# Attention feeding a hash-routed expert layer: a new start order, and one expert's gathers issued earlier

## The chip, the cores and the metric

The kernel runs on one core of a Trainium2 chip. The metric is the device time of one execution in microseconds. All times below are microseconds from the start of the profiled span unless a duration is meant. Engines: TensorE (PE in the profile; PEld is its weight load), VectorE (DVE), ScalarE (ACT), GpSimd (POOL) and SyncE (SP). POOL and SP also issue DMA transfers; those of POOL share one queue, q0.

## The reference

```python
# attention: batch 8, 12 heads, 448 tokens, head width 64
q_n, k_n = rmsnorm(q, g_q), rmsnorm(k, g_k)          # x / sqrt(mean(x*x) + 1e-6) * g
attn = softmax(q_n @ k_n.T / sqrt(64))
x = (attn @ v) as rows of 768                        # 3584 tokens
# experts: 8, width 768 -> 1024 -> 768
e = token_id * 2654435761 % 8
out[token] = relu(x[token] @ w1[e]) @ w2[e]
```

## The kernel before

**Attention.** The 96 heads are taken in 48 steps of two heads; a batch has 6 steps. A step needs the square sums of its q and k rows (`sqq`, `sqk`, then `sumq`, `sumk` on TensorE against the identity, then `redq`, `redk` on VectorE), the factor 1/rms (`ln`, `er`, two small ScalarE operations), the scaled rows (`nq`, `nk`, VectorE), their transposes (`Tq`, `Tk`, TensorE) and the copies of these into SBUF (`qT`, `kT`). Then come four score products (`sc`), four exponentials on ScalarE (`exp`), the product with v (`av`), the row sums (`rec`) and the scaling (`x`). Factors are made per group: group 0 is step 0, group 1 is steps 1 and 2, group 2 is steps 3, 4 (its first part, `sqk:2.0.0`) and 5 (`sqk:2.0.1`).

Every engine works through its instructions in program order, and that order is written out by hand: `emit` reads a text of tokens (`kind:step.part`). The first text covers batches 0 and 1, the texts `steady` and `tail` the rest. `@A` puts an operation on ScalarE, `@S` takes a score bank for a result. `spin:n` emits n products of zeros whose result nobody reads.

**The first loads.** The lines 803 to 821 issue them: step 0 over several queues, then on POOL's queue k and q of steps 1 and 2 (`load_pairs(..., 1, 0, ...)`), v of steps 0 to 2 (`load_v(0, 3)`, four transfers), k and q of steps 3 and 4, v of steps 3 to 5, and then whole batches. Step 5 comes over SP's queue (`load_one`).

**Experts.** For expert e, `gemm1` makes the hidden rows of 512 token slots and `gemm2` the output rows, tile by tile (4 tiles of 128 slots; the last has 96). The tokens of expert e are gathered from the stored attention result by `fetch(e, ...)`, four indirect transfers issued by POOL; `xg_ring` holds two experts' tokens. They are turned by TensorE (`turn`, experts 0 and 1) or by 16 VectorE instructions for a whole expert (`turn_blocks`, experts 2 to 6), which read all four tiles at once. The weights of expert 3 and later are a list of five pieces each, `queue`; `w_next` issues pieces between other work on POOL. In the loop over e the order on POOL is: `fetch(e + 2)`, pieces, then four scatters of the output, each followed by a piece:

```python
if e < E - 2:
    fetch(e + 2, range(KT))
    turn_blocks(e + 1)
gemm1(w1_view(e, w1_sb), xTs.pop(e), h_sb, 0, FIT, e >= E - 2, after)
...
(0, "k", 2): [table_mm, lambda: fetch(2, range(KT))],
```

The last line is an entry of `plan`, run behind the third tile of expert 0's `gemm2`.

Of the kernel before, what the change touches and what calls it, by code (L numbers as in the profile page):

```python
# [20 lines left out]
def kernel(  # L21
# [14 lines left out]
    B, H, S, D = q.shape  # L36
# [4 lines left out]
    HP = H // 2  # L41
# [10 lines left out]
    LAST = FIT - 3 * P  # L52
    KT = CAP // P
# [211 lines left out]
    with tc.manual_schedule(), \  # L265
# [15 lines left out]
        q_bufs = [qk_keep[0], a_nat.tile([P, RAW], FP16, name="qr_1")]  # L281
# [32 lines left out]

        def load_pairs(t, bufs, b, h, o, step, n):
            dst = raw_at(bufs, b, o, n * SL * D).rearrange("p (n r) -> p n r", n=n)
            nc.gpsimd.dma_start(out=dst, in_=bass.AP(
                tensor=t.tensor, offset=t.offset + (b * H + h) * S * D,
                ap=[[SL * D, P], [step * S * D, n], [1, SL * D]]))

        def load_v(s, n):
            b = s // HP
            o = HP * (b % 2) + s % HP
            load_heads([nc.gpsimd] * 4, v_bufs[b // 2 % NB][:, o:o + n], v, s, n)
# [480 lines left out]
        setup()  # L805
        nc.vector.memset(warm, 0.0)
        load_pairs(k, k_bufs, 0, 1, 0, HP, 2)
        make_identity(nc, ident16[:])
        load_pairs(q, q_bufs, 0, 1, 0, HP, 2)
        load_v(0, 3)  # L810
        load_pairs(k, k_bufs, 0, 3, 2 * PAIR, HP, 2)
        load_pairs(q, q_bufs, 0, 3, 2 * PAIR, HP, 2)
        load_v(3, 3)
        load(1)
        load(2, "kq")
# [72 lines left out]
        def emit(text, b):  # L888
# [15 lines left out]
                    step_ops[kind](s0 + at, *rest)  # L904

        emit("""
            zero:0 zero:1 zero:2 zero:6 zero:7 spin:11 sqk:0.0 zero:3 sqq@A:0.0 sumk@S:0.0
            redk:0.0 sumq@S:0.0 ln:0.1.2 redq:0.0 er:0.1.2 ln:0.0.1 er:0.0.1 sqk@A:1.0
            gain:0 spin:2 nk:0 spin:4 gain:1 Tk@S:0 nq:0 sumk@S:1.0 gain:2 sqq:1.0 Tq@S:0
            redk:1.0 sumq:1.0 kT:0 redq:1.0 qT@A:0 sc:0.0 ln:1 er:1 sc:0.1 spin:5 exp:0.0  # L910
            nk:1 Tk@S:1 sc:0.3 nq:1 Tq:1 sqk:2.0.0 kT:1 qT:1 exp:0.1 sqq:2.0.0 v:0
            sqk@A:2.0.1 sc:0.2 exp:0.3 sumk@S:2.0 sc:1.0 sqq@A:2.0.1 exp:0.2 exp:1.0
            sumq:2.0 redk:2.0 av:0.0 redq:2.0 sc:1.2 av:0.1 v:1 sc:1.3 ln:2 er:2 av:0.2
            sc:1.1 nq:3 rec:0 exp:1.2 exp:1.3 Tq@S:3 exp:1.1 nk:3 sc:2.0 Tk:3 x:0 exp:2.0
            sc:2.1 exp:2.1 qT:3 kT:3 sc:2.2 av:1.0 exp:2.2 sc:2.3 av:1.1 av:1.2 sqk:3.0
            sc:4.0 exp:2.3 nk:5 sumk:3.0 rec:1 exp:4.0 sc:3.0 x:1 sc:3.1 av:2.0 redk:3.0
            av:2.1 sqk:4.0 exp:3.0 nq:5 sumk:4.0 v:2 sc:3.2 av:2.2 redk:4.0 sqq:3.0 rec:2
            exp:3.1 Tk@S:5 sc:3.3 kT:5 x:2 sumq:3.0 exp:3.2 sc:4.3 sc:4.2 exp:3.3 redq:3.0
            exp:4.3 ln:3 er:3 sc:4.1 exp:4.2 av:3.0 sqk:4.1 Tq:5 exp:4.1 sqq:4.0 av:3.1 qT:5
            sumk@S:4.1 nq:6 av:3.2 nk:6 redk:4.1 sc:5.0 rec:3 sumq:4.0 sc:5.3 sc:5.1 exp:5.0  # L920
            exp:5.3 redq:4.0 sqq:4.1 x:3 Tk:6 exp:5.1 Tq@S:6 kT:6 sumq@S:4.1 redq:4.1 qT@A:6
            av:4.0 av:4.1 ln:4 sc:5.2 av:4.2 er:4 exp:5.2 sc:6.0 sqk:5.0 v:4 sc:7.0 sumk:5.0
            exp:6.0 rec:4 sc:6.3 x:4 av:5.0 av:5.1 exp:7.0 exp:6.3 nq:8 sc:7.3 redk:5.0 nk:8
            exp:7.3 v:3 Tq:8 sc:6.1 av:5.2 qT:8 sc:6.2 Tk@S:8 rec:5 sqq:5.0 exp:6.1 sc:7.1
            sumq:5.0 x:5 exp:6.2 av:6.0 sc:7.2 exp:7.1 exp:7.2 kT:8 sc:8.0 sqq:5.1 redq:5.0
            sc:8.1 nq:10 exp:8.0 av:6.1 sumq:5.1 nk:10 redq:5.1 exp:8.1 av:6.2 sc:8.3 rec:6
            Tk:10 x:6 sc:9.0 sc:8.2 exp:8.3 av:7.0 sc:9.3 exp:9.0 kT:10 Tq:10 av:7.1 av:7.2
            sc:9.1 sqk:5.1 qT:10 exp:8.2 rec:7 sc:9.2 x:7 v:5 exp:9.3 exp:9.1 sumk:5.1
            redk:5.1 exp:9.2 sqq:6.0 av:8.0 av:8.1 av:8.2 sc:10.0 sc:10.2 sc:10.1 rec:8 ln:5
            er:5 x:8 nk:12 exp:10.0 sumq:6.0 av:9.0 exp:10.1 sc:10.3 redq:6.0 Tk:12 av:9.1  # L930
            nq:12 av:9.2 kT:12 rec:9 exp:10.2 sc:11.0 exp:10.3 exp:11.0 sc:11.2 exp:11.2
            sc:11.3 x:9 Tq:12 sqq:6.1 av:10.0 av:10.1 sc:11.1 qT:12 nk:14 av:10.2 exp:11.3
            sc:12.0 sumq:6.1 sc:12.2 rec:10 exp:11.1 sc:12.1 x:10 exp:12.0 exp:12.2 redq:6.1
            Tk:14 sc:12.3 sqk:6.0 exp:12.1
        """, None)
        steady = """
            exp:0.3 av:-1.0 av:-1.1 nq:2 av:-1.2 kT:2 sc:1.0 exp:1.0 rec:-1 x:-1 Tq:2 sc:1.1
# [26 lines left out]
    with tc.manual_schedule(), \  # L964
# [83 lines left out]
        def fetch(e, kts):  # L1048
            for kt in kts:
                c = e * KT + kt  # L1050
                xgs[c] = gather(xg_ring[:, c % (2 * KT)],
                                gidx[0:P if kt < KT - 1 else LAST, c:c + 1],
                                N_EARLY if kt < KT - 1 else N)
# [4 lines left out]
            bank = ps_x.tile([P, DIN], FP16, name="xT_ps")  # L1058
            put_xT(xgs.pop(e * KT + kt), xTs[e], kt, bank[:], copy)

        def turn_blocks(e):
            xT = xTs[e] = m_x.tile([P, CO, CAP], FP16, name="xT")
            c0 = e * KT % (2 * KT)
            xg = xg_ring[:, c0:c0 + KT].rearrange("p k (c m r) -> p k m c r", m=4, r=32)
            dst = xT[:].rearrange("p c (g r) -> p c g r", r=32)
            for kt in range(KT):
                xgs.pop(e * KT + kt)
            for i in range(4):
                n = KT if 32 * i < LAST else KT - 1
                g = slice(i, i + 4 * (n - 1) + 1, 4)  # L1070
                for m in range(4):
                    nc.vector.transpose(  # L1072
                        out=dst[32 * m:32 * m + 32, :, g].rearrange("p c k r -> p k c r"),
                        in_=xg[32 * i:32 * i + 32, 0:n, m])
# [166 lines left out]
        def each(f, *parts):  # L1241
            return [lambda p=p: f(p) for p in parts]
# [3 lines left out]
            (0, "g", 4): [p7, p8], (0, "g", 5): [p9, p10, p11],  # L1246
            (0, "g", 6): each(low, 0, 1), (0, "g", 7): each(low, 2, 3), (0, "k", 0): [high],
            (0, "k", 1): [high_tok], (0, "k", 2): [table_mm, lambda: fetch(2, range(KT))],
            (1, "k", 0): [overflow_table],
        }  # L1250
        t = lambda e, kt: (lambda: turn(e, kt))
        t0 = lambda e, kt: (lambda: turn(e, kt, nc.scalar.copy))
        before, between = {}, {}
# [10 lines left out]
        for e in range(E):  # L1264
            w1_sb, w2_sb = w_tiles[e]
            h_sb = hs[e] = m_h.tile([P, FO, CAP], FP16, name="h_sb")
            after = [plan.get((e, "g", fo), []) for fo in range(FO)]
            if e == 0:
                gemm1(w1_view(e, w1_sb), xTs[e], h_sb, 0, EARLY, False, after, 2)
            else:  # L1270
                if e == E - 2:
                    turn_by_dma(E - 1)
                if e < E - 2:
                    fetch(e + 2, range(KT))
                    turn_blocks(e + 1)
                gemm1(w1_view(e, w1_sb), xTs.pop(e), h_sb, 0, FIT, e >= E - 2, after)
            if e:
                w_next(2)
            if e == 2:
                n_ov = nc.values_load(novi[0:1, 0:1], min_val=0, max_val=NOV)  # L1280
            if e == E - 1:
                nc.gpsimd.drain()
            for kt in range(KT):
                c = e * KT + kt
                for f in before.get((e, kt), []):
                    f()
                gemm2(w2_sb, h_sb, kt, gidx[:, c:c + 1], between=between.get((e, kt)),
                      last=(c == E * KT - 1), by_v=e in (0, E - 2, E - 1))
                for f in plan.get((e, "k", kt), []):
                    f()  # L1290
                if e or kt > 1:
                    w_next(1)
            w_next(len(queue))
            if e + 4 < E:
                queue += w_pieces(e + 4)
# [47 lines left out]
```

## Time and profile before

| | |
|---|---|
| median of 3 runs (lowest to highest) | 333.07 us (332.08 to 333.38) |
| the profiled execution: time, span | 332.74 us, 331.1 us |
| PE busy | 318.2 us (96%) |
| VectorE busy | 239.3 us (72%) |
| ScalarE busy | 207.5 us (63%) |
| POOL busy | 149.5 us (45%) |
| POOL's DMA queue q0 | 39072 packets, 58.32 MB |

Attention lasts to about 160 us, the experts from there to the end. Between two instructions of an engine the trace notes the idle time in brackets and what ended it, as `[0.52 <-DVE xT L1072]`. A row with `xN` merges N instructions in sequence.

### The profile page before, as it was taken

To read this page: it belongs to the slowest core of one execution; us is meant where nothing else is said; L and a number is where in the kernel's file an instruction comes from. 1 tells how busy PE (TensorE), PEld (TensorE's weight loads), DVE (VectorE), ACT (ScalarE), POOL (GpSimd) and SP (SyncE) were. 2 spreads that over 40 slices of the span, in tenths; PEclk is the share of its full clock that TensorE was granted. 3 is DMA by queue.
4 is the path that set the end of the run, shared out by engine and by line. 5 is a ranking of instruction groups with operands and counts; after the bars stand their busy time and mean duration, and the time that the engine had idled before them with its cause. 6 is when DMAs were issued, how large, how long until landed. Compare 5 with 4: busy or idle time off the path is not lost. (4 is left out here: it accounts for less than half of the span.)

```text
span 331.1 us, 8985 instructions
## 1 busy us (share of the span) xinstructions
PE 318.2 (96%) x3765; PEld 219.7 (66%) x3765; DVE 239.3 (72%) x457; ACT 207.5 (63%) x317; POOL 149.5 (45%) x207
## 2 busy tenths in 40 slices
PE   7699999999999999999999999999999999999992
PEld 3467777777777777666767766666676675766761
DVE  4689999898999999985694397693958939422210
ACT  4699999999999999999543333424334253321211
POOL 8799944432441100003475872655727556403122
PEclk9999999999999999999999999999999999999997
DMA  6999999999999999722478699999999999993013
GB/s 122 197 202 203 194 242 196 236 200 240 203 240 212 245 225 227 164 70 70 124 152 211 165 207 242 244 264 265 265 272 239 254 253 260 307 174 137 23 48 124
DMA packets 45601, 65.52 MB, mean 198 GB/s; under 512 B 12727, under 2 KB 33423, under 8 KB 45432
## 3 DMA queue, kind: packets, MB, share of 16 engines
q0 software_dynamic: 39072, 58.32, 87.7%
q1 hardware_dynamic: 6328, 6.50, 7.5%
q8 instruction: 30, 0.49, 0.6%
q10 hardware_dynamic: 160, 0.11, 0.1%
q14 instruction: 11, 0.09, 0.1%
HBM read 89.29 MB, written 17.30 MB: 322 GB/s over the span
## 5 line engine op out<-in xcount | busy, mean ns | idle before, releaser
L660 ACT ACTIVATE expT<-sc_ps 128x896 bf16<-128x896 f32 x144 | 125.1, 960 | 1.0 <-PE sc_ps L637 0.7
L1072 DVE STREAM_TRANSPOSE xT<-kr 32x768 f16<-32x768 f16 (+1 forms) x80 | 73.6, 920 | 25.7 <-DMA kr<-x_scratch,gidx 15.2
L1024 PEld LDWEIGHTS <-h_sb 128*128 128x128 f16 (+1 forms) x512 | 52.2, 104 | 31.3
L1024 PE MATMUL o_ps<-w_sb,h_sb 128*128 128x512 f16 (+3 forms) x384 | 64.2, 326 | 0.0
L1011 ACT ACTIVATE h_sb<-h_ps 128x480 f16<-128x480 f32 (+1 forms) x56 | 31.3, 560 | 48.6 <-PE h_ps L1002 48.6
L1037 POOL DMA_INDIRECT out_dram<-o_sb,gidx x32 | 35.1, 1097 | 57.6 <-ACT o_sb L1034 29.6
L1034 ACT COPY o_sb<-o_ps 128x768 f32<-128x768 f32 (+1 forms) x26 | 20.8, 799 | 54.5 <-PE o_ps L1024 54.5
L230 POOL DMA_INDIRECT kr<-x_scratch,gidx x32 | 32.6, 1020 | 49.3 <-DVE qT L629 37.1
L1002 PEld LDWEIGHTS <-w_sb 128*128 128x128 f16 x300 | 39.8, 135 | 16.4 <-issue 0.7
L1002 PE MATMUL h_ps<-xT,w_sb 128*128 128x480 f16 x240 | 49.4, 366 | 0.3 <-DVE xT L1072 0.3
L637 PE MATMUL sc_ps<-qT,kT 64*128 64x448 f16 x288 | 44.4, 356 | 0.5 <-DVE qT L629 0.4
L678 PEld LDWEIGHTS <-expT 128*128 128x128 bf16 x846 | 36.8, 97 | 9.2 <-DVE x_sb L738 4.4
L678 PE MATMUL av_ps<-v,expT 128*128 128x65 bf16 x828 | 41.5, 193 | 0.1
L306 POOL DMA_DIRECT2D vr<-in_v_dram x36 | 23.7, 670 | 20.8 <-DMA kr<-in_k_dram 11.5
L738 DVE TENSOR_TENSOR x_sb<-av_ps,srec 128x448 f16<-128x448 f32 x47 | 29.3, 623 | 1.3
L663 ACT ACTIVATE expT<-sc_ps 128x448 bf16<-128x448 f32 x48 | 28.4, 595 | 0.1
L387 PEld LDWEIGHTS <-ident 128*128 128x128 f16 x576 | 22.6, 98 | 8.7 <-issue 4.4
L683 PE MATMUL av_ps<-v,expT 128*128 128x130 bf16 x138 | 24.0, 220 | 0.0
L1024 PE MATMUL o_ps<-kr,h_sb 128*128 128x512 f16 (+3 forms) x128 | 21.1, 326 | 0.0
L1002 PE MATMUL h_ps<-xT,qr 128*128 128x480 f16 x96 | 19.8, 366 | 0.5 <-DVE xT L1072 0.5
L637 PEld LDWEIGHTS <-kT 64*128 64x128 f16 x288 | 12.3, 93 | 9.5 <-issue 2.2
L1105 POOL DMA_DIRECT2D w_sb<-in_moe_w_dram x20 | 13.7, 692 | 9.4 <-DMA w_sb<-in_moe_w_dram 6.8
(226 smaller groups left out, 409.4 us busy)
## 6 DMA issues: line engine op xcount, KB each, us to landing
w_sb<-in_moe_w_dram POOLq DMA_DIRECT2D x18, 512.0 KB, 12.5
w_sb<-in_moe_w_dram POOLq DMA_DIRECT2D x8, 768.0 KB, 12.7
kr<-in_k_dram POOLq DMA_DIRECT2D x7, 672.0 KB, 15.6
qr<-in_q_dram POOLq DMA_DIRECT2D x7, 672.0 KB, 12.9
x_scratch<-x_sb SPq DMA_DIRECT2D x15, 288.0 KB, 6.4
w_sb<-in_moe_w_dram POOLq DMA_DIRECT2D x2, 1536.0 KB, 21.3
qr<-in_moe_w_dram POOLq DMA_DIRECT2D x6, 512.0 KB, 17.6
vr<-in_v_dram POOLq DMA_DIRECT2D x14, 192.0 KB, 13.6
```

The lines of the kernel that those rows point to most:

```text
L230: nc.gpsimd.indirect_dma_start(out=xg[0:idx.shape[0], :], out_offset=None, in_=x_dram[0:rows, :], in_offset=bass.IndirectOffsetOnAxis(ap=i ...
L637: nc.tensor.matmul(sc[:, hh, :S], lhsT=kT[64 * hh:64 * hh + 64, P * j:P * j + P], rhs=qT[64 * hh:64 * hh + 64, :], start=True, stop=True)
L660: nc.scalar.activation(expT[:, 2 * j:2 * j + 2, :], sc[:, :, :S], AF.Exp, bias=0.0, scale=1.0)
L663: nc.scalar.activation(expT[:, 6, :], sc[:, 0, :S], AF.Exp, bias=0.0, scale=1.0)
L678: nc.tensor.matmul(av[:, 2 * t + hh, :], lhsT=expT[:, tl(hh, j), P * t:P * t + P], rhs=v8[:, i, vs(hh, j), 0:D + 1], start=(hh == 0 and t ...
L683: nc.tensor.matmul(av[:, 2 * t:2 * t + 2, :], lhsT=expT[:, 6, P * t:P * t + P], rhs=v8[:, i, 0::7, 0:D + 1], start=False, stop=False)
L738: nc.vector.tensor_tensor(out=xs[b][:, :, hp * D:hp * D + D], in0=av[:, :, :D], in1=srec[:, :, None].to_broadcast([P, SL, D]), op=ALU.mult)
L1002: nc.tensor.matmul(dst, lhsT=w1v[:, co, fo, :], rhs=src, start=(co == 0), stop=(co == CO - 1))
L1011: nc.scalar.activation(h_sb[:, fo, c0:c1], h_ps[:, :c1 - c0], AF.Relu)
L1024: nc.tensor.matmul(o_ps[d0 > 0][0:w, d0:d1], lhsT=h_sb[:, fo, col * P:col * P + w], rhs=w2_sb[:, fo, d0:d1], start=(fo == 0), stop=(fo == ...
L1037: scat = nc.gpsimd.indirect_dma_start(out=out[:, :], out_offset=bass.IndirectOffsetOnAxis(ap=idx[0:w], axis=0), in_=o_sb[0:w], in_offset=N ...
L1072: nc.vector.transpose(out=dst[32 * m:32 * m + 32, :, g].rearrange("p c k r -> p k c r"), in_=xg[32 * i:32 * i + 32, 0:n, m])
```

## The change

Three edits. First, the loads of q of steps 1 and 2 move ahead of the making of the identity on POOL, and k and q of steps 3 and 4 move ahead of v of steps 0 to 2. Second, the text for batches 0 and 1 is written anew: the same operations in another order, with 29 idle products in place of 22 (15 at the head in place of 11); `sqk:0.0`, and of step 6 `kT` instead of `qT`, are on ScalarE, while `sqk:1.0` and `qT:0` go from ScalarE to VectorE. Third, expert 3's four gathers move from the start of expert 1 to the end of expert 0, ahead of the four pieces of expert 3's weights that are issued there; and `turn_blocks(2)` turns three tiles, the fourth being turned by TensorE with a ScalarE copy within expert 1's `gemm2`.

```diff
         load_pairs(k, k_bufs, 0, 1, 0, HP, 2)
+        load_pairs(q, q_bufs, 0, 1, 0, HP, 2)
         make_identity(nc, ident16[:])
-        load_pairs(q, q_bufs, 0, 1, 0, HP, 2)
-        load_v(0, 3)
         load_pairs(k, k_bufs, 0, 3, 2 * PAIR, HP, 2)
         load_pairs(q, q_bufs, 0, 3, 2 * PAIR, HP, 2)
+        load_v(0, 3)
         load_v(3, 3)
...
-            zero:0 zero:1 zero:2 zero:6 zero:7 spin:11 sqk:0.0 zero:3 sqq@A:0.0 sumk@S:0.0
-            redk:0.0 sumq@S:0.0 ln:0.1.2 redq:0.0 er:0.1.2 ln:0.0.1 er:0.0.1 sqk@A:1.0
-            gain:0 spin:2 nk:0 spin:4 gain:1 Tk@S:0 nq:0 sumk@S:1.0 gain:2 sqq:1.0 Tq@S:0
-            redk:1.0 sumq:1.0 kT:0 redq:1.0 qT@A:0 sc:0.0 ln:1 er:1 sc:0.1 spin:5 exp:0.0
-            nk:1 Tk@S:1 sc:0.3 nq:1 Tq:1 sqk:2.0.0 kT:1 qT:1 exp:0.1 sqq:2.0.0 v:0
-            sqk@A:2.0.1 sc:0.2 exp:0.3 sumk@S:2.0 sc:1.0 sqq@A:2.0.1 exp:0.2 exp:1.0
-            sumq:2.0 redk:2.0 av:0.0 redq:2.0 sc:1.2 av:0.1 v:1 sc:1.3 ln:2 er:2 av:0.2
...
+            zero:0 zero:1 zero:2 zero:6 zero:7 spin:15 zero:3 sqk@A:0.0 gain:0 sumk@S:0.0
+            sqq@A:0.0 redk:0.0 sumq:0.0 ln:0.1.2 gain:1 spin:4 redq:0.0 er:0.1.2 nk:0 Tk@S:0
+            ln:0.0.1 er:0.0.1 gain:2 spin:1 nq:0 Tq@S:0 sqk:1.0 kT:0 spin:2 qT:0 sumk@S:1.0
+            sqq:1.0 sc:0.0 sc:0.2 sumq:1.0 exp:0.0 redk:1.0 redq:1.0 ln:1 sqk:2.0.0 er:1
+            spin:7 sc:0.3 sqk@A:2.0.1 sumk@S:2.0 exp:0.2 nq:1 nk:1 sqq:2.0.0 exp:0.3
+            sqq@A:2.0.1 redk:2.0 Tq:1 Tk@S:1 qT:1 kT:1 sc:0.1 exp:0.1 sumq@S:2.0 sc:1.0
+            redq:2.0 sc:1.1 sc:2.0 ln:2 v:0 av:0.0 er:2 nq:3 v:1 exp:1.0 exp:1.1 av:0.1 Tq:3
...
-        def turn_blocks(e):
+        def turn_blocks(e, tiles=KT):
...
-            for kt in range(KT):
+            for kt in range(tiles):
                 xgs.pop(e * KT + kt)
             for i in range(4):
-                n = KT if 32 * i < LAST else KT - 1
+                n = tiles if 32 * i < LAST else min(tiles, KT - 1)
...
             (0, "k", 1): [high_tok], (0, "k", 2): [table_mm, lambda: fetch(2, range(KT))],
+            (0, "k", 3): [lambda: fetch(3, range(KT))],
...
+        before[1, 2] = [t0(2, KT - 1)]
...
                 if e < E - 2:
-                    fetch(e + 2, range(KT))
-                    turn_blocks(e + 1)
+                    if e > 1:
+                        fetch(e + 2, range(KT))
+                    turn_blocks(e + 1, KT if e > 1 else KT - 1)
```

## Rows read from the trace of the kernel before

**Rows 1.** Windows: busy time of each engine, granted clock, DMA share, GB/s.

```profile
60.00:80.00 20.00, 20.00 (x368) 14.54 (x365) 18.67 (x39) 20.00 (x33) 6.81 (x10) 1.00 1.28 231
240.00:260.00 20.00, 20.00 (x113) 13.42 (x112) 14.55 (x17) 7.58 (x13) 11.40 (x14) 1.00 1.07 256
```

**Rows 2.** Timeline, 0 to 22 us: start, duration, engine, line, operation.

```profile
1.41 4.29 PE L827 MATMUL av_ps<-hi 128*128 128x448 f16 x11 [1.41 <-DVE hi L806]
...
6.24 0.57 PE L387 MATMUL sc_ps<-sq_k,ident 128*128 128x32 f16 x16 [0.53 <-DVE sq_k L375]
...
7.57 1.28 DVE L435 TENSOR_TENSOR n_one<-expT,rr 128x512 f16<-128x512 f32 x2
...
10.77 0.63 DVE L375 TENSOR_TENSOR sq_q<-qr 128x896 f16<-128x896 f16 x1 [1.85 <-DMA qr<-in_q_dram]
...
11.44 0.47 DVE L626 TENSOR_SCALAR kT<-sc_ps,g_col 128x512 f16<-128x512 f16 x1
...
12.31 0.23 ACT L406 ACTIVATE ss<-ss 128x28 f32<-128x28 f32 x1 [1.87 <-DVE ss L402]
...
12.85 0.63 DVE L435 TENSOR_TENSOR n_k<-kr,rr 128x896 f16<-128x896 f16 x1 [0.57 <-ACT rr L412]
...
15.23 0.75 DVE L626 TENSOR_SCALAR kT<-sc_ps,g_col 128x1024 f16<-128x1024 f16 x1
...
17.17 0.92 ACT L660 ACTIVATE expT<-sc_ps 128x896 bf16<-128x896 f32 x1 [0.46 <-PE sc_ps L637]
...
18.75 0.90 ACT L660 ACTIVATE expT<-sc_ps 128x896 bf16<-128x896 f32 x1
```

**Rows 3.** DMA view, 0 to 8.5 and 0 to 10.5 us: packets, MB of q0.

```profile
q0 software_dynamic: 624, 0.66, 50.4%
...
q0 software_dynamic: 1147, 0.90, 59.1%
```

**Rows 4.** DMA issues, 4 to 5 and 7 to 8 us: size, us to landing.

```profile
qr<-in_q_dram POOLq DMA_DIRECT2D x1, 224.0 KB, 6.5
...
kr<-in_k_dram POOLq DMA_DIRECT2D x1, 224.0 KB, 7.3
```

**Rows 5.** Timeline, 196 to 331 us: first products of experts 2, 3, 5, 6, 7.

```profile
203.75 9.88 PE L1002 MATMUL h_ps<-xT,qr 128*128 128x480 f16 x48 [0.52 <-DVE xT L1072]
...
224.37 9.88 PE L1002 MATMUL h_ps<-xT,w_sb 128*128 128x480 f16 x48 [0.34 <-DVE xT L1072]
...
264.72 9.88 PE L1002 MATMUL h_ps<-xT,w_sb 128*128 128x480 f16 x48
...
284.86 9.88 PE L1002 MATMUL h_ps<-xT,qr 128*128 128x480 f16 x48
...
304.98 9.88 PE L1002 MATMUL h_ps<-xT,w_sb 128*128 128x480 f16 x48
```

**Rows 6.** Timeline of VectorE, 245 to 290 us: turning experts 5 and 6.

```profile
249.75 14.92 DVE L1072 STREAM_TRANSPOSE xT<-kr 32x768 f16<-32x768 f16 x16 [5.25 <-PE h_ps L1002]
269.89 14.92 DVE L1072 STREAM_TRANSPOSE xT<-kr 32x768 f16<-32x768 f16 x16 [5.22 <-DMA kr<-x_scratch,gidx]
```

**Rows 7.** Timeline of POOL: pieces of expert 3, then its first and fourth gather.

```profile
186.85 0.81 POOL L1105 DMA_DIRECT2D w_sb<-in_moe_w_dram  x1
...
188.94 2.63 POOL L1105 DMA_DIRECT2D w_sb<-in_moe_w_dram  x4
191.87 1.08 POOL L230 DMA_INDIRECT kr<-x_scratch,gidx  x1 [0.30 <-issue]
...
195.88 0.99 POOL L230 DMA_INDIRECT kr<-x_scratch,gidx  x1 [0.30 <-issue]
```

**Rows 8.** DMA issues, 218.9 to 220 us: the last gather of expert 4.

```profile
kr<-x_scratch,gidx POOLq DMA_INDIRECT x1, 10.5
```

**Rows 9.** DMA view, 186 to 196 us: busy tenths in 40 slices of 0.25 us.

```profile
DMA  0955409329900999999998999799998999999999
```

**Rows 10.** DMA view, 226.5 to 229.5 us, when expert 4's gathers move.

```profile
DMA packets 342, 0.79 MB, mean 264 GB/s; under 512 B 42, under 2 KB 42, under 8 KB 341
```

More of the change, by code (lines that the diff above doesn't have):

```diff
@@ L913 @@
-            sumq:2.0 redk:2.0 av:0.0 redq:2.0 sc:1.2 av:0.1 v:1 sc:1.3 ln:2 er:2 av:0.2
[L914 to L934, printed above, removed]
+            zero:0 zero:1 zero:2 zero:6 zero:7 spin:15 zero:3 sqk@A:0.0 gain:0 sumk@S:0.0
+            sqq@A:0.0 redk:0.0 sumq:0.0 ln:0.1.2 gain:1 spin:4 redq:0.0 er:0.1.2 nk:0 Tk@S:0
@@ new lines @@
+            ln:0.0.1 er:0.0.1 gain:2 spin:1 nq:0 Tq@S:0 sqk:1.0 kT:0 spin:2 qT:0 sumk@S:1.0
[3 more added lines that the diff above has]
+            redq:2.0 sc:1.1 sc:2.0 ln:2 v:0 av:0.0 er:2 nq:3 v:1 exp:1.0 exp:1.1 av:0.1 Tq:3
+            av:0.2 nk:3 sc:1.2 exp:2.0 exp:1.2 sc:1.3 qT:3 Tk:3 exp:1.3 rec:0 x:0 sc:2.1
@@ new lines @@
+            sc:2.2 nk:5 av:1.0 exp:2.1 kT:3 sqk:3.0 v:2 exp:2.2 av:1.1 sc:2.3 Tk:5 sc:3.0
+            av:1.2 kT:5 exp:2.3 rec:1 x:1 sc:3.2 sc:3.1 sumk:3.0 nq:5 exp:3.0 av:2.0 exp:3.2
+            redk:3.0 av:2.1 exp:3.1 sqk:4.0 Tq:5 sc:4.0 exp:4.0 qT:5 sqq:3.0 sc:4.2 av:2.2
+            sumk:4.0 rec:2 x:2 exp:4.2 redk:4.0 sumq@S:3.0 sc:3.3 redq:3.0 av:3.0 sc:4.1
+            exp:3.3 sc:5.0 sqq:4.0 sc:5.2 ln:3 er:3 sumq:4.0 exp:4.1 exp:5.0 av:3.1 sqk:4.1
+            nk:6 sc:5.3 redq:4.0 v:3 sqq:4.1 sumk:4.1 av:3.2 exp:5.2 redk:4.1 sc:4.3
@@ new lines @@
+            sumq:4.1 rec:3 Tk@S:6 exp:5.3 nq:6 Tq@S:6 redq:4.1 x:3 qT:6 exp:4.3 sc:5.1
+            sqk:5.0 av:4.0 av:4.1 ln:4 kT@A:6 av:4.2 sc:6.0 sc:6.2 er:4 exp:5.1 exp:6.0
+            sumk:5.0 nk:8 rec:4 sc:6.1 x:4 exp:6.2 sc:7.0 redk:5.0 Tk:8 exp:6.1 exp:7.0
+            av:5.0 nq:8 av:5.1 av:5.2 Tq@S:8 kT:8 sqq:5.0 sc:7.3 sc:6.3 rec:5 exp:7.3 qT:8
+            sumq:5.0 x:5 exp:6.3 sc:8.0 sc:7.2 sc:7.1 redq:5.0 sqq:5.1 av:6.0 exp:8.0
+            exp:7.2 av:6.1 sumq:5.1 sc:8.3 nq:10 av:6.2 sc:9.0 exp:7.1 nk:10 redq:5.1 Tk:10
@@ new lines @@
+            exp:8.3 sc:8.1 v:4 rec:6 exp:9.0 x:6 sc:8.2 kT:10 av:7.0 av:7.1 Tq:10 exp:8.1
+            sc:9.3 sqk:5.1 exp:8.2 av:7.2 qT:10 rec:7 x:7 v:5 exp:9.3 sc:9.1 sc:9.2 sumk:5.1
+            exp:9.1 av:8.0 redk:5.1 av:8.1 exp:9.2 av:8.2 sc:10.0 sc:10.2 sqq:6.0 rec:8 ln:5
+            er:5 x:8 exp:10.0 sumq:6.0 nk:12 redq:6.0 av:9.0 sqq:6.1 sc:10.1 nq:12 sc:10.3
+            Tk:12 exp:10.2 av:9.1 sc:11.0 av:9.2 kT:12 exp:10.1 sc:11.2 exp:10.3 rec:9
+            exp:11.0 sc:11.1 Tq:12 exp:11.1 exp:11.2 sc:11.3 x:9 qT:12 exp:11.3 sqk:6.0
@@ L935 @@
+            av:10.0 av:10.1 nk:14 sumq:6.1 redq:6.1 sc:12.0 av:10.2 exp:12.0 rec:10 sc:12.2
+            exp:12.2 sc:12.1 Tk:14 sc:12.3 exp:12.1 x:10
         """, None)
```

## The prediction

> **What bounds the kernel now.** I read the windows first, stage by stage. In attention ScalarE is busy 20.00 of 20 us [rows 1]: the exponentials set the pace, and a better start is worth only as much ScalarE idle time as it takes out. From about 188 us the experts run, TensorE is busy 20.00 of 20 us, and the DMA engines show a share of 1.07 [rows 1]. Both look full, so the question is which leads.
>
> The timelines answer it. An expert that waits for nothing takes 20.12 us (284.86 to 304.98) [rows 5]. VectorE finishes turning expert 5 at 249.75 + 14.92 = 264.67 and expert 6 at 269.89 + 14.92 = 284.81 [rows 6]; TensorE begins these experts at 264.72 and 284.86 [rows 5]. Twice the gap is 0.05 us: TensorE starts when the turned tokens are there, though it is idle so briefly that no wait is printed. VectorE in turn had been idle for 5.2 us and was released, in the second row, by the gathers' landing [rows 6]. The 5.25 us of the first row are put down to TensorE's product, but I take them for the same wait, since the period between the two starts is 20.14 us. And a gather lands 10.5 us after its issue [rows 8], behind the weights in the same queue. So from expert 4 on the chain is: DMA queue, gather, VectorE, TensorE. Its pace (224.37 to 264.72 is 40.35 us for two experts, 20.18 each) is only just above TensorE's own 20.12.
>
> Visible waits are left at expert 2, 0.52 us, and expert 3, printed as 0.34 us [rows 5]; by the starts, expert 2 to 3 took 20.62, so 0.50 us over 20.12.
>
> **The start.** In the kernel before, VectorE waits 1.85 us for q of steps 1 and 2, until 10.77, with `kT:0` queued behind the square; `kT:0` starts at 11.44 and ScalarE's steady work (`ln:1`) at 12.31 [rows 2]. The new text puts `kT:0` and `qT:0` ahead of that square.
>
> *Idle products.* The 11 products fill 4.29 us from 1.41, so 0.37 us each after the first's latency, the 1.2 GHz level for 448 columns, and the sums start at 6.24 [rows 2]. Four more cost between 4 x 0.19 (at 2.4 GHz) and 4 x 0.37 us, so they end between about 6.3 and 7.0; I take 6.6, step 0 starting 0.4 us later. The gap up to 6.24 covers the rest. The other idle products sit where TensorE waits for VectorE, and cost nothing as long as it does; if not, 7 of them are 1.3 us at 0.19.
>
> *Step 0.* VectorE scaled step 0 until 7.57 + 1.28 = 8.85 [rows 2], so now until about 9.3. Then come `sqk:1.0` (0.63, as the square row), `kT:0` (0.47) and `qT:0` (at most the same) [rows 2]: 9.3 + 0.63 + 0.47 + 0.47 = 10.9, and after the products the first exponential at about 11.4. Moving `sqk:0.0` to ScalarE frees VectorE while it was waiting for data anyway.
>
> *Loads.* q of steps 1 and 2 is issued about 0.6 us earlier, ahead of the identity, but what the queue carries up to this transfer's end is 224 KB each for step 0's q, the k pair and the q pair, 0.69 MB, and it has moved 0.66 MB by 8.5 us [rows 3]; the transfer landed at 4.26 + 6.5 = 10.76 [rows 4], some 2 us after its bytes. The queue sets this, so I give the earlier issue nothing (at best the 0.6). k of steps 3 and 4 now has 0.92 MB up to its end, reached just after 10.5 us [rows 3]; with a lag of about 2 us it lands at 12.3 to 12.8 in place of 7.40 + 7.3 = 14.70 [rows 4]. v of steps 0 to 2 lands some 2 us later than it did; its first use, behind `redq:2.0`, comes at about 17 us, which covers it. Bytes ahead of batch 1 are the same.
>
> *Step 1.* The square of q starts at about 10.95 (10.77 before), so `ln:1` comes 1.54 us later as before, at 12.5. VectorE takes `sqk:2.0.0` first, at 12.5 to 12.8, then scales step 1 from 13.15 or 13.45 for 1.26 us, to 14.4 or 14.7. Ahead of the copies stand the square of q (0.63) and a reduction (0.24, an estimate from the 0.23 of the small rows): 15.3 to 15.6. Two copies of at most 0.75 [rows 2] end at 16.8 to 17.1. Then `redq:2.0`, `ln:2`, `er:2` at about 0.25 each, and `exp:1.0` starts at 17.5 to 17.8. It ends, at 0.84 apart, by 18.35 to 18.65. In the kernel before, the same set of ScalarE work is done at 18.75 [rows 2]. That gains 0.1 to 0.4 us. If products and copies overlap better (copies of 0.6, k landed at 12.3, step 0 at 6.3), it gains 1.05; had ScalarE no idle time at all after an exponential at 10.9, against 12.31 and a wait of 0.46 [rows 2], it would gain 12.31 + 0.46 - 10.9 = 1.9, so 2 us is the bound. For a loss, the same k at a landing 1 us later gives +0.7. I take **-0.6 us**, from +0.7 to -2. Step 6's `kT` for `qT` on ScalarE, 1024 columns for 896, adds at most 0.1, in that range.
>
> **The experts.** *What is removed:* the 0.52 and 0.50 us at experts 2 and 3. *Added:* six transposes of 96 columns on TensorE, at the price of a product row (9.88 / 48 = 0.21 us for 480 columns [rows 5]) 0.25 us, and a ScalarE copy in a stage where ScalarE is 38% busy. VectorE turns three tiles for four, so it ends early, and expert 3's tokens are there long before. Taken alone: 1.02 - 0.25 = 0.8 us won up to expert 3.
>
> *What is moved:* four gathers on POOL. They start 1.34 us apart ((195.88 - 191.87) / 3 [rows 7]), so the four big pieces behind them are issued 5.35 us later, at 194.3 in place of 188.94. In the kernel before the gathers were issued while those pieces kept the DMA engines full; now they are issued with little in the queue. The first piece, issued at 186.85, begins to move at 189.25, where the zeros end [rows 7, 9], so 2.40 us after issue; moved pieces then start at 196.7. Ahead of them lie: that first piece, 512 KB at the 0.2 MB/us of this stretch, 2.6 us; a scatter of 288 KB, 1.1 us at 264 GB/s; four gathers, 720 KB, 2.8 us at that rate [rows 10]. From 189.25 this is done at 195.75. So the engines stand idle 0.95 us that they worked before. If gathers move faster, 2.1 us, and the scatter 0.75, the idle time is 2.0 us. I take 1.5. The bytes ahead of expert 4's gathers are the same as before, the queue is full from there on [rows 1], so these land **1.5 us later**, VectorE turns later, and expert 4 starts 1.5 us later than it did. The 0.8 us won up to expert 3 turns into a longer wait there: won time is not kept, and lost queue time is.
>
> One rule bears on this. The Trainium skill, "DMA: Bandwidth & Descriptors", section "Anatomy of one DMA - SWDGE (gpsimd) path", fits a POOL transfer as a fixed 2.0 us plus its bytes at 436 KB per us, with half of the rate reached only near 860 KB, which speaks against putting four small transfers where nothing else moves. By that rate, an estimate, the four gathers need 1.7 us of movement, the idle time becomes 0.95 + 1.1 = 2.05 us, and the time 334.5. In this trace the 264 GB/s of rows 10 is below the page's rate, and the sum stays with the row.
>
> **Sum.** -0.6 + 1.5 = +0.9 us against the profiled execution, 332.74 to 333.64. That execution lies 0.33 under the median of the runs, so for a median I add 0.9 to 333.07: **334.0 us**. A change of 0.5% (1.67 us) is about what can be told from none.
>
> **Rivals.**
> *The queue has slack.* If the DMA engines can make up 1.5 us by expert 4 or 5, TensorE leads, the experts win 0.8 us and another 0.1 at 4 to 6, and with the start -1.5: 331.6, or 331.1 with the better start. For it: 20.18 is close to 20.12, and a full share need not be a full rate. Against it: gathers land 10.5 us after issue [rows 8], which an unfilled queue would not show. It decides from the point where the pace of the queue is under 20.0 us. Chance 0.28.
> *The move is neutral.* The queue leads, but the idle time is filled because earlier data or the scatter take longer: expert 4 starts as before, nothing lost or kept. -0.6: 332.5. Chance 0.15.
> *The start loses.* k of steps 3 and 4 lands a microsecond later, VectorE stands in front of it with step 1's scaling behind: +0.7 + 1.5, so 335.3. Against it is the byte count [rows 3]. Chance 0.15.
> The forecast has 0.42.
>
> **How the numbers follow.** Faster by over 0.5% (under 331.4) takes half of the first rival (0.15), a part of the second with a start near -2 (0.05), and a little of the forecast: 0.22. Slower (over 334.74) takes the last rival (0.13) and a fifth of the forecast with idle time and start at the bad ends (0.09): 0.22. The rest is 0.56. The range runs from the first rival with its better start, 331.1, to the last rival, 335.4. Both signs hold much of the chance; the forecast's own range is 333.0 to 335.0, from -1.05 + 1.0 to -0.1 + 2.0.
>
> **What would show it.** Right: `kT:0` on VectorE by 10.5; `sqk:2.0.0` by 13; ScalarE without a gap after about 17.5. Among the experts: no wait at expert 3, DMA slices below full between 192 and 197 (shifted with attention), and a TensorE wait of 2 to 3 us at expert 4 behind VectorE. Wrong: TensorE going through experts 2 to 6 at 20.12 with no wait; or a start where ScalarE has more idle time after its first exponential than the kernel before.

## The result, and the profile after

The changed kernel takes **336.41 us** (median of 6 runs, 334.58 to 337.19) beside 332.79 us for the kernel before (332.08 to 333.49, 6 runs): ratio 1.0098, interval 1.0069 to 1.0128. It is slower by 1%, and outside the predicted range of 331.1 to 335.4. The profiled execution took 336.74 us with a span of 334.9, 3.8 us longer than the span of before. Executions more than 1.5% above the fastest of their kernel count in no median or ratio below (two of 12 in the third experiment, two of seven in the sixth, three of 12 in the seventh).

The timeline of TensorE shows where the time went. These are the first products of experts 2 to 7 in the changed kernel, which answer to [rows 5]:

```profile
202.78 9.88 PE L1002 MATMUL h_ps<-xT,qr 128*128 128x480 f16 x48
222.90 3.81 PE L1002 MATMUL h_ps<-xT,w_sb 128*128 128x480 f16 x18
226.97 6.24 PE L1002 MATMUL h_ps<-xT,w_sb 128*128 128x480 f16 x30 [0.27 <-ACT h_sb L1011]
246.90 11.39 PE L1002 MATMUL h_ps<-xT,w_sb 128*128 128x480 f16 x48 [3.29 <-DVE xT L1072]
268.53 9.88 PE L1002 MATMUL h_ps<-xT,w_sb 128*128 128x480 f16 x48
288.65 9.88 PE L1002 MATMUL h_ps<-xT,qr 128*128 128x480 f16 x48
308.77 9.88 PE L1002 MATMUL h_ps<-xT,w_sb 128*128 128x480 f16 x48
```

In the kernel before expert 4 began without a printed wait:

```profile
244.55 9.88 PE L1002 MATMUL h_ps<-xT,w_sb 128*128 128x480 f16 x48
```

The waits at experts 2 and 3 are gone, and they start 0.97 and 1.47 us earlier than before [rows 5]. Expert 4 then waits 3.29 us for VectorE, and its 48 products take 11.39 us in place of 9.88. Its start is 2.35 us later than before. Expert 5 starts at 268.53, in place of 264.72 [rows 5]: 3.81 us later, and that is the whole loss. From there on every expert again takes 20.12 us, with no wait.

VectorE was late at expert 4 because the gathers were. Its row for expert 4 before, then its rows for experts 4 to 6 in the changed kernel, which answer to [rows 6]:

```profile
229.58 14.92 DVE L1072 STREAM_TRANSPOSE xT<-kr 32x768 f16<-32x768 f16 x16 [5.26 <-DMA kr<-x_scratch,gidx]
```

```profile
231.93 14.91 DVE L1072 STREAM_TRANSPOSE xT<-kr 32x768 f16<-32x768 f16 x16 [15.96 <-DMA kr<-x_scratch,gidx]
252.53 14.91 DVE L1072 STREAM_TRANSPOSE xT<-kr 32x768 f16<-32x768 f16 x16 [5.69 <-DMA kr<-x_scratch,gidx]
272.81 14.92 DVE L1072 STREAM_TRANSPOSE xT<-kr 32x768 f16<-32x768 f16 x16 [5.36 <-DMA kr<-x_scratch,gidx]
```

Changed, it ends expert 4 at 246.84 and TensorE starts at 246.90. But it ends expert 6 at 287.73, 0.92 us ahead of TensorE: by then TensorE leads, and what it lost at expert 4 is not made up.

POOL's timeline, for [rows 7], shows the order of issue. The second block is the kernel before, its first gather of expert 4:

```profile
186.33 0.80 POOL L1105 DMA_DIRECT2D w_sb<-in_moe_w_dram  x1
...
188.73 1.05 POOL L230 DMA_INDIRECT kr<-x_scratch,gidx  x1 [0.30 <-issue]
...
192.69 0.98 POOL L230 DMA_INDIRECT kr<-x_scratch,gidx  x1 [0.30 <-issue]
193.68 4.13 POOL L1105 DMA_DIRECT2D w_sb<-in_moe_w_dram  x6
...
217.40 1.06 POOL L230 DMA_INDIRECT kr<-x_scratch,gidx  x1 [3.00 <-DMA w_sb<-in_moe_w_dram]
```

```profile
214.77 1.06 POOL L230 DMA_INDIRECT kr<-x_scratch,gidx  x1 [1.38 <-DMA w_sb<-in_moe_w_dram]
```

Expert 3's four gathers stand first, the pieces follow at 193.68, and the first gather of expert 4 is issued at 217.40. That is 2.63 us later than before, after a longer wait that the trace puts down to a weight transfer: the delay is there at the issue already. The windows view (columns as in rows 1) shows what the new order did to the DMA engines and to TensorE's clock; the first row is the kernel before, the others the changed one:

```profile
192.00:196.00 4.00, 4.00 (x25) 2.32 (x23) 3.95 (x5) 1.33 (x3) 3.08 (x4) 1.00 1.07 205
```

```profile
192.00:194.00 2.00, 2.00 (x12) 0.94 (x11) 1.97 (x3) 0.57 (x1) 1.69 (x3) 1.00 0.76 260
194.00:196.00 2.00, 2.00 (x15) 1.23 (x13) 1.96 (x4) 0.80 (x1) 2.00 (x4) 1.00 0.63 115
...
246.00:248.00 2.00, 1.10 (x3) 0.47 (x3) 0.83 (x2) 0.80 (x1) 1.17 (x2) 0.65 0.97 294
248.00:250.00 2.00, 2.00 (x6) 0.83 (x5) 0.00 (x0) 0.51 (x1) 0.00 (x0) 0.50 1.05 300
```

The DMA share falls to 0.76 and 0.63 where it was 1.07 before, with the engines full [rows 9]. And the granted clock falls to 0.50, the 1.2 GHz level, as expert 4 begins. Over a longer stretch the loss of the queue is read in GB/s. First the kernel before, then the changed one:

```profile
186.00:220.00 34.00, 33.48 (x185) 21.89 (x184) 26.49 (x30) 12.93 (x21) 20.94 (x24) 1.00 1.03 222
```

```profile
186.00:220.00 34.00, 34.00 (x196) 22.41 (x194) 28.06 (x35) 13.31 (x21) 18.33 (x22) 1.00 0.99 209
```

13 GB/s over 34 us are 0.44 MB that were not moved by 220 us, or 2.0 us at 222 GB/s.

The start, for [rows 2]: VectorE's timeline, then ScalarE's, both of the changed kernel.

```profile
9.00 0.48 DVE L626 TENSOR_SCALAR kT<-sc_ps,g_col 128x512 f16<-128x512 f16 x1
...
9.69 0.62 DVE L375 TENSOR_TENSOR sq_q<-qr 128x896 f16<-128x896 f16 x1
...
11.10 0.62 DVE L375 TENSOR_TENSOR sq_k<-kr 128x896 f16<-128x896 f16 x1
...
20.67 0.63 DVE L375 TENSOR_TENSOR sq_k<-kr 128x896 f16<-128x896 f16 x1 [0.75 <-DMA kr<-in_k_dram]
```

```profile
10.23 0.92 ACT L660 ACTIVATE expT<-sc_ps 128x896 bf16<-128x896 f32 x1 [2.57 <-PE sc_ps L637]
...
15.73 3.32 ACT L660 ACTIVATE expT<-sc_ps 128x896 bf16<-128x896 f32 x4
...
24.83 1.73 ACT L660 ACTIVATE expT<-sc_ps 128x896 bf16<-128x896 f32 x2 [0.86 <-PE sc_ps L637]
...
36.75 0.98 ACT L663 ACTIVATE expT<-sc_ps 128x448 bf16<-128x448 f32 x2 [0.68 <-PE sc_ps L640]
37.90 2.54 ACT L660 ACTIVATE expT<-sc_ps 128x896 bf16<-128x896 f32 x3 [0.18 <-PE sc_ps L637]
```

`exp:1.0` starts at 15.73, so the set of ScalarE work that was done at 18.75 [rows 2] is done at 15.73 + 0.84 = 16.57, 2.2 us earlier. Then VectorE waits 0.75 us for k of batch 1, and ScalarE has idle times of 0.86, 0.68 and 0.18 us that the kernel before did not have. At its last exponential it is 0.89 us ahead (157.29 in place of 158.18), and at its next work, a copy for the experts that waits for TensorE, 0.54 us (158.91 in place of 159.45). Last, one row of the view by line: the first products whose weights lie in `w_sb` (experts 1, 3, 4, 5 and 7), start of the first and of the last, before and after.

```profile
L1002 PE MATMUL h_ps<-xT,w_sb x240: 363/366/366, 182.9 to 314.5; 128*128 128x480 f16 x120
```

```profile
L1002 PE MATMUL h_ps<-xT,w_sb x240: 365/367/605, 182.4 to 318.3; 128*128 128x480 f16 x120
```

The first of the two times is the start of expert 1: 0.5 us earlier. From it to the second were 131.6 us and are 135.9. So the change loses 4.3 us among the experts and wins 0.5 ahead of them. The longest product, 605 ns in place of 366, is one at the lower clock.

### The profile page after: what moved, and what is told of

It reads as the page before. It is cut to its first block, busy times and chain, and to the rows that moved or that the text cites. A ratio compares the mean times of both kernels' runs of the same rounds, so it can differ in the third digit from the quotient of the medians.

```text
span 334.9 us, 9012 instructions
## 1 busy us (share of the span) xinstructions
PE 320.5 (96%) x3778; PEld 220.9 (66%) x3778; DVE 237.2 (71%) x458; ACT 206.7 (62%) x317; POOL 147.7 (44%) x207
## 5 line engine op out<-in xcount | busy, mean ns | idle before, releaser
L1072 DVE STREAM_TRANSPOSE xT<-kr 32x768 f16<-32x768 f16 (+1 forms) x80 | 71.2, 890 | 31.9 <-DMA kr<-x_scratch,gidx 30.8
L1002 PE MATMUL h_ps<-xT,w_sb 128*128 128x480 f16 x240 | 51.1, 374 | 3.6 <-DVE xT L1072 3.3
L678 PE MATMUL av_ps<-v,expT 128*128 128x65 bf16 x828 | 40.8, 193 | 0.4 <-DVE x_sb L738 0.2
## 6 DMA issues: line engine op xcount, KB each, us to landing
qr<-in_moe_w_dram POOLq DMA_DIRECT2D x6, 512.0 KB, 17.5
```

What stands on the lines that cost most here:

```text
L678: nc.tensor.matmul(av[:, 2 * t + hh, :], lhsT=expT[:, tl(hh, j), P * t:P * t + P], rhs=v8[:, i, vs(hh, j), 0:D + 1], start=(hh == 0 and t ...
L1002: nc.tensor.matmul(dst, lhsT=w1v[:, co, fo, :], rhs=src, start=(co == 0), stop=(co == CO - 1))
L1072: nc.vector.transpose(out=dst[32 * m:32 * m + 32, :, g].rearrange("p c k r -> p k c r"), in_=xg[32 * i:32 * i + 32, 0:n, m])
```

## The experiments

The theory after the result: the gathers ahead of the weight pieces cost the queue about 2 us and more, expert 4 waits, the clock falls in that wait, and the start is worth little. The rivals: the start itself, or the TensorE tile, does the harm; or late scatters, for want of output buffers, do. Times are medians; the ratio, with its 95% interval, is to the kernel before in runs on the same chip, and is not the quotient of two medians.

**Start alone.** Only the first two edits; the experts are those of the kernel before.

```diff
         load_pairs(k, k_bufs, 0, 1, 0, HP, 2)
+        load_pairs(q, q_bufs, 0, 1, 0, HP, 2)
...
+            zero:0 zero:1 zero:2 zero:6 zero:7 spin:15 zero:3 sqk@A:0.0 gain:0 sumk@S:0.0
```

> The start alone (loads and first text of the changed kernel), experts as in the kernel before. Theory 1, the experts lose the time: attention ends 0.54 us earlier as in the changed kernel's profile, so 0.3 to 0.9 us faster than before (0.2%). Rival, the new order of the start loses it: 2 us or more slower.

332.72 us, ratio 1.0008 (0.9981 to 1.0035): no gain that can be measured, where one was expected. The start does no harm either.

**The move alone.** The kernel before with expert 3's gathers ahead of the pieces.

```diff
+            (0, "k", 3): [lambda: fetch(3, range(KT))],
...
-                    fetch(e + 2, range(KT))
+                    if e > 1:
+                        fetch(e + 2, range(KT))
```

> Only expert 3's gathers moved ahead of the four weight pieces; start and turning as before. Theory 1, idle time of the DMA queue reaches TensorE at expert 4: expert 4 starts about 2.9 us later than before, so 2.9 us slower if the clock stays at 2.4 GHz through the wait and up to 3.9 us if it falls as in the changed kernel (1.46 us over expert 4, of which the queue would have taken 0.6 anyway). Rival, the tile turned by TensorE or the start is the cause: within 0.5 us of before.

335.34 us, ratio 1.0093 (1.0062 to 1.0125): the move alone is the loss. In its timeline expert 4 waits too:

```profile
246.14 9.88 PE L1002 MATMUL h_ps<-xT,w_sb 128*128 128x480 f16 x48 [2.47 <-DVE xT L1072]
```

In this execution the products kept 9.88 us, and the granted clock stayed at 1.00 from 246 to 250 us. From the start of expert 1 to that of expert 4 it took 63.79 us, in place of 61.61: 2.2 us of delay with no part of the other edits in it. The 12 runs go from 333.21 to 338.17; the profile is of a run of 334.34. The runs fall into two groups by the mean granted clock of the whole execution: six at 0.995 to 0.998 took 333.21 to 334.87 us, and six at 0.985 to 0.993 took 335.82 to 338.17.

**Start and TensorE tile, without the move.**

```diff
-            (0, "k", 3): [lambda: fetch(3, range(KT))],
...
-                    if e > 1:
-                        fetch(e + 2, range(KT))
+                    fetch(e + 2, range(KT))
```

> The changed kernel with expert 3's gathers back behind the weights. Theory 1, the queue leads from expert 4 on: no wait at expert 2, the won time waits at expert 3 or 4, expert 4 starts as before counted from the end of attention, and only the 0.5 us of the start is left. Rival, the queue has slack and TensorE leads: 0.5 us more from expert 2, so 1.0 us or more faster than before.

332.68 us, ratio 1.0005 (0.9977 to 1.0032). Expert 2 starts with no wait, and expert 3 waits 0.90 us, expert 4 0.17: what the tile wins is waited for again, as long as the gathers stand where they stood.

**The clock kept up.** The changed kernel with 14 idle products of 448 columns on TensorE behind expert 3's work, into a bank that nobody reads.

```diff
+                if e == 3 and kt == KT - 1:
+                    idle = ps_h.tile([P, 512], FP32, name="h_ps")
+                    for _ in range(14):
+                        nc.tensor.matmul(idle[:, 0:448], lhsT=ident16[:],
+                                         rhs=hi1[:].rearrange("p c a -> p (c a)")[:, 0:448],
+                                         start=True, stop=True)
```

> The changed kernel with 14 idle products on TensorE behind expert 3, 2.6 us at 2.4 GHz, inside the wait of 3.3 us before expert 4. Theory 1 with the clock as a second cost: expert 4's products run at 2.4 GHz throughout, experts 4 to 5 take 1.46 us less, but then wait for the queue at experts 5 and 6, so the end comes 0.9 us earlier than in the changed kernel. Rival, TensorE leads behind expert 4: 1.46 us earlier. Rival, the wait alone is the cost and the clock falls regardless: no change.

335.53 us (333.99 to 335.89), ratio 1.0089 (1.0062 to 1.0117). The median is 0.88 us less than that of the changed kernel, but the ratio only 0.0009, or 0.3 us. The timeline shows the products in the wait, and expert 4 at full clock:

```profile
242.82 2.81 PE L1297 MATMUL h_ps<-hi,ident 128*128 128x448 f16 x14
246.00 2.19 PE L1002 MATMUL h_ps<-xT,w_sb 128*128 128x480 f16 x10 [0.37 <-DVE xT L1072]
```

The delay up to expert 4 is 2.2 us here, as with the move alone. Runs whose ranges overlap and intervals of 0.3% do not settle what the clock is worth in the median; that products at the lower clock were slow, and at the kept clock were not, the rows show.

**Two pieces ahead of the gathers.** The changed kernel, with two of the four pieces issued first.

```diff
-            (0, "k", 3): [lambda: fetch(3, range(KT))],
+            (0, "k", 3): [lambda: w_next(2), lambda: fetch(3, range(KT))],
```

> The changed kernel, but expert 3's gathers stand behind two of the four weight pieces, so that 1 MB keeps the DMA engines full while POOL issues them. Theory 1, the loss is idle time of the DMA queue: no slices below full behind 189 us, expert 4's last gather lands as early as in the kernel before, the wait at expert 4 is about 1 us, the clock stays, and the time is that of the kernel before within 0.6 us, 3 us less than the changed kernel. Rival, the bytes of the gathers ahead of the weights are the loss, idle or not: still 2 us or more slower than before.

334.09 us beside 333.71, ratio 1.0013 (0.9995 to 1.0031): no loss is left that can be measured. The DMA view of 186 to 196 us, first of the changed kernel and then of this one (tenths, 0.25 us each; for [rows 9]):

```profile
DMA  1850742890179999999999997989394734542994
```

```profile
DMA  3085740942495069999999988999799999999999
```

The hole near 194 us is filled. From 186 to 220 us this kernel moves 222 GB/s as the kernel before does, and expert 4's wait falls from 3.29 to 1.01 us. Its first gather of expert 4 is issued at 215.00, beside 214.77 before and 217.40 in the changed kernel. That is the cleanest test of the queue's step: the same gathers and weights, with two pieces moved ahead of the gathers.

**All gathers ahead of scatters and weights.** On top of that, the gathers of experts 4 to 7 are issued behind the first scatter of the expert three places ahead.

```diff
-            (1, "k", 0): [overflow_table],
+            (1, "k", 0): [overflow_table, lambda: fetch(4, range(KT))],
+            **{(x, "k", 0): [lambda x=x: fetch(x + 3, range(KT))] for x in range(2, E - 3)},
...
-        before[1, 2] = [t0(2, KT - 1)]
+        before[1, 0] = [t0(2, KT - 1)]
...
-                    if e > 1:
-                        fetch(e + 2, range(KT))
```

> As the run before, and the gathers of experts 4 to 7 are each issued behind the first scatter of the expert two or three ahead of them, so ahead of three of its weight pieces. Theory 1, TensorE starts experts late only because gathers stand behind weights in a queue that is always full: VectorE turns early, experts 2 to 6 follow each other at 20.12 us with no wait, and 1.0 to 1.2 us are won against the kernel before (331.4). Rival, the queue then brings the weights late and TensorE waits for them: no gain, or slower.

337.29 us (five runs), ratio 1.0097 (1.0059 to 1.0136): a miss. Experts 2 and 3 take 20.12 us and no expert waits for VectorE, but later ScalarE stands still, and TensorE behind it:

```profile
291.27 0.79 ACT L1034 COPY o_sb<-o_ps 96x768 f32<-96x768 f32 x1 [6.49 <-DMA out_dram<-o_sb,gidx]
```

```profile
292.59 7.83 PE L1002 MATMUL h_ps<-xT,qr 128*128 128x480 f16 x30 [2.45 <-ACT h_sb L1011]
```

ScalarE waits for a scatter to free one of the five output buffers. The same with the old start:

> The same expert stage behind the start of the kernel before. Theory 1: 1.0 to 1.2 us faster than before; against the run with the new start it tells what that start is worth once the experts keep what they are given: 0.5 us by the one profile, nothing by the timed run of the start alone.

337.20 us (nine runs), ratio 1.0091 (1.006 to 1.0123): within intervals of 0.3 to 0.4% the start makes no difference there. The runs fall into two groups again: four at a granted clock of 0.994 to 0.996 took 334.26 to 335.01 us, five at 0.986 to 0.991 took 337.20 to 338.57.

**k of batch 1 earlier.** Start alone, with this load ahead of v of steps 3 to 5.

```diff
+        load(1, "k")
         load_v(3, 3)
-        load(1)
+        load(1, "qv")
```

> The start alone with the experts of the kernel before, and k of batch 1 loaded ahead of v of steps 3 to 5. Theory, what the new start wins by 16 us (2.1 us of ScalarE time) is given back because VectorE comes to the square of batch 1's k before it has landed: it lands about 1.7 us earlier, ScalarE's wait near 25 us goes, attention ends 0.5 to 0.9 us earlier than with the start alone. Rival, v of steps 3 to 5 is late instead, or the next batch's loads set the pace: no change against the start alone.

333.21 us, ratio 0.9991 (0.9972 to 1.0009). ScalarE's idle time near 25 us is gone, but expert 1 starts at 182.4 and no gain is measured.

**Eight output buffers in place of five.** Four kernels: the one before, the changed one, the one with all gathers first, the one with two pieces first.

```diff
-         tc.tile_pool(name="m_o", bufs=5) as m_o, \
+         tc.tile_pool(name="m_o", bufs=8) as m_o, \
```

> The kernel before with 8 output buffers in place of 5, and nothing else. If the buffers do not bind where the gathers are issued behind the weights, it is the same: 332.3 to 333.3 us beside 332.8. If waits for output buffers cost the kernel before too, up to 1 us less.

332.92 us, ratio 1.0004 (0.9985 to 1.0024): no difference.

> The changed kernel with 8 output buffers. Theory 1, the loss comes from the queue's idle time ahead of expert 4's gathers and the clock's fall in that wait: no gain, 336 to 336.8 us. Rival, ScalarE's 3.81 us wait for an output buffer near 226 us is what delays the expert before: then about 0.3 to 1 us less, up to 335.4.

336.14 us, ratio 1.0092 (1.0063 to 1.0121): ScalarE's waits for output buffers are gone from its trace, the loss is not. Expert 4 waits 3.32 us and its products take 11.45 us. Late scatters are not the cause.

> All gathers ahead of the scatters and weights, as in the sixth run (337.7 us), with 8 output buffers. If the queue held that kernel only through the five output buffers, TensorE now goes through the experts at 20.12 us with no wait and the time is 331.0 to 332.3 us, faster than both. Rival, the queue's bytes per expert bind: the wait moves on to the weights or to the eight buffers, and the time stays at 333 us or more.

**331.03 us, ratio 0.9943 (0.9926 to 0.9960)**: faster than both. The same row of first products as above, and the windows row of the queue:

```profile
L1002 PE MATMUL h_ps<-xT,w_sb x240: 366/366/366, 181.5 to 312.0; 128*128 128x480 f16 x120
```

```profile
186.00:220.00 34.00, 34.00 (x196) 22.47 (x195) 31.52 (x39) 12.78 (x21) 21.65 (x26) 1.00 1.04 233
```

From expert 1 to the last product it takes 130.5 us, with no wait at any of experts 2 to 7, 1.1 us less than before. The queue moves 233 GB/s, more than the 222 of before.

> The fifth run (334.1 us: gathers of expert 3 behind two of the four weight pieces) with 8 output buffers. If the gathers' place behind the weights of each expert sets the pace, it is unchanged, 333.5 to 334.5 us; if late scatters held ScalarE and so TensorE, about 0.5 us less.

332.55 us, ratio 1.0001 (0.9974 to 1.0027): expert 4 still waits 0.93 us, and eight buffers alone do not bring the gain of the run before, which differs from this one by the place of the gathers of experts 4 to 7 and by the point at which TensorE turns its tile of expert 2.

**What the start is worth where no queue wait is left.** The fastest kernel with the old start, and with k of batch 1 ahead.

> The eleventh run (331.0 us, no wait among the experts) with the start of the kernel before. If the start's step of -0.6 us is real and was only hidden by the queue in the other runs, this is 0.5 to 0.7 us slower than the eleventh run: 331.5 to 331.8 us. Rival, the new start is worth nothing: 330.8 to 331.2 us.

331.65 us beside 333.42, ratio 0.9945 (0.9915 to 0.9975).

> The eleventh run with the load of k of batch 1 issued ahead of v of steps 3 to 5, so that the idle time after the first exponentials goes. If ScalarE's idle time near 25 us is what gives the start's gain back, up to 0.9 us less than the eleventh run: 330.1 to 330.8 us. Rival, attention is paced by the loads as a whole and the idle time moves on: 330.8 to 331.3 us.

331.73 us, ratio 0.9941 (0.9915 to 0.9967). Against 0.9943 with the new start, all three are the same within the intervals of some 0.3%, 1 us. With the old start that row of first products goes from 182.6 to 313.1: again 130.5 us.

## Why the prediction was wrong, point by point

**Which leads: half right.** That TensorE starts experts 4 to 6 when turned tokens arrive, and that time won up to expert 3 is not kept there, was right: start and tile without the move show it. That the queue's pace is what binds was not. With the gathers ahead and eight output buffers the queue brings the same weights and tokens in time, and no expert from 3 on starts later than 20.12 us after the one before. What bound was the gathers' place behind weights and scatters. So the rival "the queue has slack" was wrong for this change and right of the queue.

**The removed waits: right.** Experts 2 and 3 start with no wait. Expert 3 starts 1.47 us earlier, 0.54 of it won ahead of the experts, so 0.93 here; foretold was 0.8.

**The queue's idle time: right in kind, too small.** The step put four gathers with little behind them, an idle time of 0.95 to 2.0 us, and took 1.5. The slices below full do lie between 193 and 197 us, as foretold. In 192 to 196 us the share is (0.76 + 0.63) / 2 = 0.70 in place of 1.07, which is 1.4 us of full work, and 1.6 us with the microsecond behind it, where it is 0.90. But the share does not hold all of the loss: by 220 us the bytes are 2.0 us behind, and expert 4's delay, counted from the start of expert 1, is 2.2 us (move alone, clock kept), 2.5 (eight buffers) and 2.89 in the profile after (64.50 in place of 61.61). The upper bound was too low; what makes the difference of 0.7 us between executions stays open.

What the step had wrong is how the gathers move. It let them follow piece and scatter without a gap, at 264 GB/s, until 195.75. The DMA view of 186 to 196 us (GB/s in slices of 0.25 us, changed kernel) shows two stretches instead:

```profile
GB/s 55 332 193 0 148 184 92 49 98 0 25 147 172 213 205 197 172 164 213 188 172 361 365 377 299 338 344 350 92 184 160 314 111 105 166 172 74 111 109 76
```

From 191.25 to 193 us it is 299 to 377 GB/s, and from there to 196, but for one slice, 74 to 184. POOL issues a gather of 192 KB every 1.3 us, the last at 192.69, which makes some 150 GB/s: the slow end looks like gathers that move as they are issued, with nothing else to move beside them. No run changed that pace, so this is a reading and not shown.

By the rate that the Trainium skill, "DMA: Bandwidth & Descriptors", section "Anatomy of one DMA - SWDGE (gpsimd) path", gives, the prediction had worked out 2.05 us, an estimate. The 2.0 us of the bytes agree with it better than with the 1.5 that the sum took, though neither has the slow end.

**The clock: left out.** The prediction foretold a TensorE wait of 2 to 3 us at expert 4 and put only its length into the sum. In the profile after, expert 4 then starts at 0.65 and 0.50 of the clock and takes 21.63 us (246.90 to 268.53), where 20.17 was to be had (244.55 to 264.72 before): 1.46 us. Not all of it counts at the end: VectorE ends expert 6 only 0.92 us ahead of TensorE, so at full clock and with the same gathers at most 0.92 us would have been won. Keeping the clock up gave 0.88 us in the medians and 0.3 us by the ratios.

On this bears the Trainium skill, "TensorE: Matmul & The Clock Gate", section "HAM oscillation — how this bites in real kernels": a wait for data in front of a block of products lets the clock fall, and the block starts cold. The trace after agrees, with 0.50 behind a wait of 3.29 us; in the move alone the clock stayed at 1.00 behind a wait of 2.47 us.

How much of the median loss is the clock's stays open. In the move alone the six runs at the higher clock lose 1.7 us to the kernel before (medians 334.33 and 332.58), near the 1.5 of the sum, and the six at the lower one 4.1. That gap of 2.4 us is more than the 1.46 us, so the fall at one expert does not account for it. And there are runs that do not fit: the changed kernel has one of 337.19 us at a granted clock of 0.999, and with the clock kept up the median loss is still 2.9 us.

**The start: the steps right, the sum not to be measured.** `kT:0` starts at 9.00 (foretold by 10.5), `sqk:2.0.0` at 11.10 (by 13). That the earlier issue of q is worth nothing was wrong: it landed 4.7 us after its issue at 3.68, at 8.4, in place of 10.76 [rows 4]. So ScalarE was 2.2 us ahead by 16.6, more than the bound of 2. But VectorE had to wait for the next data in the queue, k of batch 1, and ScalarE's idle times of 1.7 us took most of the lead back; "ScalarE without a gap after 17.5" was wrong. That the -0.54 in the profile is close to the -0.6 is luck, by errors that cancel: executions with the old start differ by as much, and the times show nothing of it (1.0008 alone, 0.9945 against 0.9943). Expert 1 started between 181.5 and 184.3 us in nine profiles with this start, and with the old one at 182.3 to 182.9 in four and at 184.6 in a fifth. Why removing the idle time near 25 us changed nothing either stays open.

**The sum.** -0.54 + 2.89 + 1.46 = +3.81, which is the span's growth; foretold was -0.6 + 1.5 = +0.9. Of the 2.9 us between them the queue's term has 1.4, the clock 1.46. So the step that failed is the price of expert 4's wait: the queue's idle time, put at 1.5 us and at most 2.0, was 2.2 to 2.9, and the slow products behind the wait were put at nothing. "The start loses" gave 335.3, the nearest time of the four, for a cause that did not happen: `sqk:2.0.0` was not late, and the start alone cost nothing.

The fastest kernel is 1.8 us under the one before, of which its profile explains 1.1 among the experts; its runs (330.26 to 331.71) also lie closer together than those of before (331.87 to 334.55). That gathers landing just in time make some executions of the kernel before wait longer than the profiled one would explain the rest, but no run shows it.

## What to carry to other kernels

Where an engine waits for small transfers that share a queue with big ones, ask first where in the queue they stand and only then how many bytes it carries: the same bytes in another order gave 1.0098, 1.0013 and, with three more output buffers, 0.9943 of the time before. Here the small transfers needed big ones in front of them to keep the DMA engines busy, and moving them all ahead made the scatters late, so the buffers behind those had to be counted too. When a prediction contains a TensorE wait of some microseconds, price the products behind it at both clock levels.

## What the runs showed of the hardware

- After a wait of 3.29 us TensorE's granted clock was 0.65, then 0.50, and 48 products took 11.39 us in place of 9.88; after one of 2.47 us in another kernel it stayed at 1.00. With fourteen idle products in the wait it was 1.00 as well.
- Near the hole in the queue the idle DMA share (1.6 us) understated the bytes that were missing 24 us later (2.0 us).
- POOL issued indirect gathers 1.3 us apart. With one piece of 512 KB issued shortly ahead of them the DMA share fell to 0.63 from 194 to 196 us; with three it was 1.06.
- All gathers first took 337.29 us with five output buffers (1.0097) and 331.03 with eight (0.9943), while eight buffers changed nothing in the kernel before (1.0004) or in the changed one (1.0092 beside 1.0098).
